# Dense layer with squared ReLU on one core: the blocks in another order, and two small weight loads on another queue

## The chip, the cores and the metric

The kernel runs on one core of one Trainium2 chip. The metric is device time in microseconds (us). "Before" had 293.56 us (median of 3 runs, 293.25 to 294.12) when the prediction was made.

## The reference

For x of 2048 x 576, w1 of 576 x 4608 and w2 of 4608 x 576, all bfloat16:

```python
h = jnp.einsum("bsd,df->bsf", x, w1) + b1
r = jnp.where(h > 0, h, 0)
h = r * r
out = jnp.einsum("bsf,fd->bsd", h, w2) + b2
```

## The kernel before

The 2048 rows are taken in four blocks of 512. For a block, stage A computes h transposed (36 column tiles of 128), and stage B multiplies it with w2. The contraction of A is 576 = 4.5 x 128. So 32 of the 36 tiles use **row-tiled** matmuls: the 128 rows of the array are two halves of 64, and two matmuls (a *pair*, lines 173 and 175) run side by side. The other four tiles use **full-array** matmuls (line 194) and a small row-tiled remainder (lines 188 and 190), whose weights are `w1n8`. B is full-array (line 233). In the profile's lines `w1_h`, the weights of the row-tiled tiles, appears as `w_h`, `w1n8` as `w1n_89` and the transposed x as `xTw`; PE are TensorE's matmuls, PEld its weight loads, DVE is VectorE, ACT ScalarE, POOL GpSimd. Before the first full-array matmul, TensorE runs seven warm-up matmuls and twenty small ones that transpose block 0 of x.

```python
    def load_w1n8(eng, h):                                   # 32 KB each
        src = w1[NK * P:D, 0:GW].rearrange("p (i h f) -> p i h f", h=2, f=P)
        keep(eng.dma_start(out=w1n8[h * H:(h + 1) * H, :, :], in_=src[:, :, h, :]))
    ...
    for k in range(NK):
        load_w1n(nc.sync, k)
    load_w1n8(nc.sync, 0)
    load_w1n8(nc.sync, 1)
    ...
    def a_full(sb, order):
        ...                      # "rows_first": remainder pairs, then the full-array groups
        ...                      # otherwise: full-array groups, then the remainder pairs
    ...
    for (j0, j1) in [(0, 1), (1, 2), (2, 4), (4, 6), (6, 8), (8, 10), (10, 12)]:
        load_w1(nc.sync, 0, j0, j1)          # upper halves of w_h, then lower halves
        load_w1(nc.sync, 1, j0, j1)
    load_xT(1)
    for (j0, j1) in [(12, 14), (14, 16)]:
        load_w1(nc.sync, 0, j0, j1)
        load_w1(nc.sync, 1, j0, j1)
    ...
    for c in (0, 3, 1, 4, 2, 5):
        load_w2(c)
    load_xT(2)

    alloc_hT(0)
    a_full(0, "k_outer")
    a_rows(0, 12, 1)
    alloc_hT(1)
    load_xT(3)
    a_rows(1)
    a_full(1, "rows_first")
    phase_b(0, hTs[0], dups=(2, 3))
    alloc_hT(2)
    a_full(2, "g_outer")
    a_rows(2)
    phase_b(1, hTs[1])
    alloc_hT(3)
    a_full(3, "g_outer")
    a_rows(3)
    phase_b(2, hTs[2])
    phase_b(3, hTs[3], last=True)
```

## Time and profile before

| what | before |
|---|---|
| span of the profiled run | 291.4 us |
| TensorE busy | 286.5 us, 98% |
| ScalarE, VectorE busy | 32%, 28% |
| first full-array matmul starts | 5.46 us |
| last matmul ends | 287.70 us |
| from there to the end of the span | 3.67 us |

The page of before, parts 1 (busy us, share of the span, instructions) and 4 (the chain of waits that ended last, by engine and by line):

```profile
PE 286.5 (98%) x2412; PEld 177.5 (61%) x2412; DVE 81.4 (28%) x189; ACT 93.7 (32%) x154; POOL 1.5 (1%) x8
...
PE 98%; ACT 0%; DVE 0%; issue 0%
```

TensorE has work nearly all the time, and the chain is its own sequence of matmuls.

The windows view of before gives one stage per line. Columns: stretch, its length, then busy time and instructions for each engine, granted clock, DMA share, GB/s. In order: blocks 0 and 1 of stage A, block 2 of A, block 3 of A, and what follows the last matmul.

```profile
5.46:76.07 70.61, 70.58 (x618) 31.39 (x619) 32.64 (x75) 45.10 (x73) 0.00 (x0) 1.00 0.83 174
...
111.35:146.51 35.16, 35.16 (x310) 15.60 (x307) 15.30 (x36) 21.32 (x34) 0.00 (x0) 1.00 0.02 6
...
181.80:216.97 35.17, 35.17 (x310) 15.60 (x308) 15.29 (x36) 21.32 (x34) 0.00 (x0) 1.00 0.02 5
...
287.70:291.37 3.67, 0.00 (x1) 0.00 (x0) 0.46 (x1) 0.00 (x0) 0.00 (x0) 0.91 0.07 22
```

Blocks 2 and 3 of A take 70.33 us together. They run apart, with a stage B between them.

The timeline of before, PE only (start, duration, line, operation), at a change from row-tiled to full-array and at one from row-tiled to stage B:

```profile
72.08 0.38 PE L188 MATMUL pn<-xTw,w1n_89 64*128 64x512 bf16 x1
72.29 0.38 PE L190 MATMUL pn<-xTw,w1n_89 64*128 64x512 bf16 x1
72.60 0.39 PE L194 MATMUL pn<-xTw,w1n 128*128 128x512 bf16 x1
...
146.20 0.38 PE L173 MATMUL ph<-xTw,w_h 64*128 64x512 bf16 x1
146.21 0.38 PE L175 MATMUL ph<-xTw,w_h 64*128 64x512 bf16 x1
146.51 0.30 PE L233 MATMUL po<-w_sb,hT 128*128 128x288 bf16 x1
```

Read the starts, not the durations, since matmuls overlap. Two starts of one half of the array are normally 0.215 us apart; across a change of mode it is 0.31 us.

The same view at the one visible wait for a weight load:

```profile
13.17 0.38 PE L173 MATMUL ph<-xTw,w_h 64*128 64x512 bf16 x1
13.18 0.38 PE L175 MATMUL ph<-xTw,w_h 64*128 64x512 bf16 x1
13.39 0.38 PE L173 MATMUL ph<-xTw,w_h 64*128 64x512 bf16 x1
13.79 0.39 PE L175 MATMUL ph<-xTw,w_h 64*128 64x512 bf16 x1
13.80 0.39 PE L173 MATMUL ph<-xTw,w_h 64*128 64x512 bf16 x1
```

At 13.39 one half of the array starts and its partner waits until 13.79.

The timeline of before, queue of SyncE (SPq), start and time over which the issues ran:

```profile
1.65 1.85 SPq L73 DMA_DIRECT2D w1n<-in_w_dram  x4
3.68 1.36 SPq L77 DMA_DIRECT2D w1n_89<-in_w_dram  x2
5.08 9.13 SPq L80 DMA_DIRECT2D w_h<-in_w_dram  x11
```

The two remainder loads take 1.36 us of issuing ahead of the first w_h load.

### The profile page before, as it was taken

What the parts mean: (1) busy time and instruction counts of PE and PEld (TensorE: products, weight loads), DVE (VectorE), ACT (ScalarE), POOL (GpSimd) and SP (SyncE); (2) the same over time, 40 slices, a digit from 0 to 9 for tenths busy, and PEclk for the clock granted to TensorE, in tenths of its full rate; (3) what the DMA queues carried; (4) which work ended last, traced back from release to release, by engine and by line L of the source; (5) the groups of instructions that cost most, each with busy time, mean ns of one, the idle gap of its engine ahead of it and who ended that gap; (6) DMA issues with size and microseconds to landing.
All of it is one profiled execution on the core that took longest, in us unless ns stands there. A gap on an engine that the chain in (4) does not pass through costs nothing.

```text
span 291.4 us, 5457 instructions
## 1 busy us (share of the span) xinstructions
PE 286.5 (98%) x2412; PEld 177.5 (61%) x2412; DVE 81.4 (28%) x189; ACT 93.7 (32%) x154; POOL 1.5 (1%) x8
## 2 busy tenths in 40 slices
PE   8999999999999999999999999999999999999994
PEld 4444444444687875444477877444457878777783
DVE  3444544444531011544411110344440111110110
ACT  4666666666400001766620000466660000000000
POOL 2000000000000000000000000000000000000000
PEclk9999999999999999999999999999999999999999
DMA  6999999900000000000000000000000000000000
GB/s 183 201 200 175 233 358 326 158 7 2 0 23 0 23 20 20 2 1 2 2 0 20 23 3 20 20 2 0 2 0 2 20 24 20 23 0 23 20 23 21
DMA packets 27320, 16.05 MB, mean 55 GB/s; under 512 B 11284, under 2 KB 27296, under 8 KB 27296
## 3 DMA queue, kind: packets, MB, share of 16 engines
q1 hardware_dynamic: 26976, 15.39, 23.2%
q8 instruction: 19, 0.31, 0.4%
q10 hardware_dynamic: 288, 0.30, 0.3%
q14 instruction: 5, 0.04, 0.0%
q0 software_dynamic: 32, 0.01, 0.0%
HBM read 11.36 MB, written 2.36 MB: 47 GB/s over the span
## 4 chain that ended last, share of the span: by engine, by line
PE 98%; ACT 0%; DVE 0%; issue 0%
PE po L233 49%; PE ph L173 23%; PE ph L175 20%; PE pn L194 5%; PE wps L61 1%; PE pn L188 1%; ACT xTw L143 0%; ACT xTw L144 0%; DVE o_sb L242 0%; PE pn L190 0%; PE ta L138 0%; PE tb L141 0%; PE tb L142 0%; PE b1T_ps L151 0%
## 5 line engine op out<-in xcount | busy, mean ns | idle before, releaser
L233 PE MATMUL po<-w_sb,hT 128*128 128x288 bf16 x1152 | 141.6, 286 | 0.0
L233 PEld LDWEIGHTS <-hT 128*128 128x128 bf16 x1152 | 112.6, 98 | 29.3 <-issue 0.8
L175 PE MATMUL ph<-xTw,w_h 64*128 64x512 bf16 x576 | 125.0, 376 | 0.0
L173 PE MATMUL ph<-xTw,w_h 64*128 64x512 bf16 x576 | 125.0, 376 | 0.0
L161 ACT ACTIVATE r<-ph,b1T 128x512 bf16<-128x512 f32 x128 | 81.1, 685 | 41.0 <-PE ph L173 20.5
L162 DVE TENSOR_TENSOR hT<-r 128x512 bf16<-128x512 bf16 x144 | 61.2, 425 | 79.3 <-ACT r L161 79.3
L173 PEld LDWEIGHTS <-w_h 64*128 64x128 bf16 x576 | 54.0, 94 | 36.4
L175 PEld LDWEIGHTS <-w_h 64*128 64x128 bf16 x576 | 54.0, 94 | 32.3 <-DMA w_h<-in_w_dram 0.8
L242 DVE TENSOR_TENSOR o_sb<-po,b_bc 128x288 bf16<-128x288 f32 x32 | 13.2, 453 | 122.5 <-PE po L233 122.5
L161 ACT ACTIVATE r<-pn,b1T 128x512 bf16<-128x512 f32 x16 | 10.0, 688 | 80.9 <-PE pn L190 80.1
L194 PE MATMUL pn<-xTw,w1n 128*128 128x512 bf16 x64 | 14.5, 379 | 0.4 <-ACT xTw L144 0.4
L194 PEld LDWEIGHTS <-w1n 128*128 128x128 bf16 x64 | 6.1, 98 | 7.6 <-DMA w1n<-in_w_dram 0.6
L61 PE MATMUL wps<-const-bfloat16-1.0 128*128 128x512 bf16 (+1 forms) x7 | 2.9, 593 | 0.8 <-PEq L306 0.8
L113 DVE COPY xTw<-xTw 64x2048 bf16<-64x2048 bf16 x4 | 2.8, 688 | 0.5 <-ACT xTw L144 0.4
L114 DVE COPY xTw<-xTw 64x2048 bf16<-64x2048 bf16 x4 | 2.8, 688 | 0.1
L188 PE MATMUL pn<-xTw,w1n_89 64*128 64x512 bf16 x8 | 2.4, 380 | 0.0
L190 PE MATMUL pn<-xTw,w1n_89 64*128 64x512 bf16 x8 | 2.4, 380 | 0.0
L139 DVE COPY xTw<-ta 128x384 bf16<-128x384 bf16 x4 | 1.2, 358 | 4.1 <-PE ta L138 4.1
L61 PEld LDWEIGHTS <-const-bfloat16-1.0 128*128 128x128 bf16 x7 | 0.9, 135 | 2.1 <-issue 2.1
L98 ACT ACT_TABLE_LOAD x1 | 1.3, 1283 | 1.7 <-PEq L306 1.7
L143 ACT COPY xTw<-tb 128x128 bf16<-128x128 bf16 x4 | 1.2, 298 | 1.1 <-PE tb L142 1.1
L138 PE MATMUL ta<-ident,x_sb 128*128 128x128 bf16 x12 | 1.4, 240 | 0.0
(20 smaller groups left out, 8.4 us busy)
## 6 DMA issues: line engine op xcount, KB each, us to landing
w_sb<-in_w_dram SPq DMA_DIRECT2D x6, 864.0 KB, 11.5
w_h<-in_w_dram SPq DMA_DIRECT2D x14, 288.0 KB, 6.7
out_dram<-o_sb SPq DMA_DIRECT2D x15, 144.0 KB, 1.8
w_h<-in_w_dram SPq DMA_DIRECT2D x4, 144.0 KB, 3.4
w1n<-in_w_dram SPq DMA_DIRECT2D x4, 128.0 KB, 3.3
x_sb<-in_x_dram ACTq DMA_DIRECT2D x2, 144.0 KB, 3.1
x_sb<-in_x_dram SPq DMA_DIRECT2D x2, 144.0 KB, 2.8
b_bc<-in_b_dram SPq DMA_DIRECT2D x1, 144.0 KB, 6.1
```

What stands on the lines that cost most here:

```text
L61: keep(nc.tensor.matmul(wps[:, 0:n], lhsT=ones[:, 0:P], rhs=ones[:, 0:n], start=True, stop=True))
L113: keep(nc.vector.tensor_copy(out=xT[0:H, SPC:SPC + 4, :], in_=xT[H:P, E3:E3 + 4, :]))
L114: keep(nc.vector.tensor_copy(out=xT[H:P, SPC:SPC + 4, :], in_=xT[0:H, O:O + 4, :]))
L161: keep(nc.scalar.activation(out=r[:], in_=bank[:], func=ACT.Relu, bias=b1T[:, ft:ft + 1], scale=1.0))
L162: keep(nc.vector.tensor_tensor(out=hTs[sb][:, ft, :], in0=r[:], in1=r[:], op=ALU.mult))
L173: keep(nc.tensor.matmul(bx[:], lhsT=w1_h[0:H, LO_C[i], jc], rhs=xT[0:H, LO_W[i], :], start=(i == 0), stop=(i == NC - 1)))
L175: keep(nc.tensor.matmul(by[:], lhsT=w1_h[H:P, UP_C[i], jc], rhs=xT[H:P, UP_W[i], :], start=(i == 0), stop=(i == NC - 1)))
L188: keep(nc.tensor.matmul(banks[2 * i][:], lhsT=w1n8[0:H, i, :], rhs=xT[0:H, SPC, :], start=start, stop=stop))
L190: keep(nc.tensor.matmul(banks[2 * i + 1][:], lhsT=w1n8[H:P, i, :], rhs=xT[H:P, E3, :], start=start, stop=stop))
L194: keep(nc.tensor.matmul(banks[g][:], lhsT=w1n[:, k, g * P:(g + 1) * P], rhs=xT[:, O + k, :], start=start, stop=stop))
L233: keep(nc.tensor.matmul(po[h][:, 0:DH], lhsT=hT[:, ft, jj * P:(jj + 1) * P], rhs=w2_sb[:, ft, h * DH:(h + 1) * DH], start=(i == 0), stop=( ...
L242: keep(nc.vector.tensor_tensor(out=o_sb[:, h * DH:(h + 1) * DH], in0=po[h][:, 0:DH], in1=b2_bc[:, h * DH:(h + 1) * DH], op=ALU.add,))
```

## The change

The intent: blocks go A0 A1 B0 B1 A2 A3 B2 B3, so that the row-tiled parts of A2 and A3 meet and full-array work stands at every border to stage B. That is four changes of tiling mode instead of six. The two remainder loads go to the GpSimd queue, so that w_h can be issued earlier.

```diff
-    load_w1n8(nc.sync, 0)
-    load_w1n8(nc.sync, 1)
 ...
     nc.gpsimd.dma_start(out=b1_rows[0:NFT, :], in_=b1.rearrange("(ft p) -> ft p", p=P))
+    load_w1n8(nc.gpsimd, 0)
+    load_w1n8(nc.gpsimd, 1)
 ...
     phase_b(0, hTs[0], dups=(2, 3))
+    phase_b(1, hTs[1])
     alloc_hT(2)
     a_full(2, "g_outer")
     a_rows(2)
-    phase_b(1, hTs[1])
     alloc_hT(3)
-    a_full(3, "g_outer")
     a_rows(3)
+    a_full(3, "rows_first")
     phase_b(2, hTs[2])
```

## The prediction

> **What bounds the kernel now.** TensorE. The busy table has PE at 286.5 us of a 291.4 us span (98%), and the chain of waits is 98% PE: second phase (L233) 49%, row-tiled first phase (L173/L175) 43%, full-array first phase (L194) 5%. Clock granted 0.999. In the timeline the matmul starts follow without holes: 0.215 us for each full 512-column matmul and for each row-tiled pair, 0.122 us for each 288-column one. ACT (32%) and DVE (28%) have slack. The change keeps all 2412 matmuls, so only holes count.
>
> **Holes that the timeline shows.**
> 1. Changes between row-tiled (64x128) and full-array matmuls. Last row pair of A1 at 72.29, first full one at 72.60: 0.31 us against 0.215. The same 0.31 us from full to row in A0, A2 and A3 (185.04 to 185.35), and from the rows of A2 and A3 to phase B (146.21 to 146.51; 216.66 to 216.97). Each is 0.095 us too long, and the next one or two starts are some 0.01 us late: about 0.10 us a change, six changes in all. Between full groups and phase B nothing is lost. This agrees with the Trainium skill, "TensorEngine Tiling (Array Packing)", Key Properties: changing the tiling mode drains the engine.
> 2. One DMA wait: at 13.39 the next pair starts 0.40 us later, waiting for a w1 load (w_h), a loss of 0.19 us.
>
> **What the change does.**
> - Order. A2 full, rows, then A3 rows, full joins the two row parts and ends with full groups before B2. It removes three switches (A2 rows to B1; A3 full to rows; A3 rows to B2) and adds one (A3 rows to A3 full). Net two fewer: 2 x 0.10 = 0.20 us, all on the critical path. Nothing new waits: hT 3 reuses the buffer B1 has finished with, x blocks 2 and 3 are ready, and eviction (0.69 us each, two per 1.94 us of rows) keeps up as from A0 to A1.
> - Loads. The two 32 KB loads cost the sync queue 1.36 us of issue (3.68 to 5.04), ahead of the first w_h issue at 5.08. Without them w_h issues start about 1.4 us sooner. The Trainium skill, "DMA: Bandwidth & Descriptors", says that issuing engines share the same 16 DMA engines and that spreading only saves issue time; issue time is what is saved here. I expect the wait at 13.39 to go: -0.19 us. On the GpSimd queue the loads are issued after the b1 load (1.45, 0.66 us), at about 2.1 and 3; with the b1 load's 3.5 us to landing they are there by about 7, needed at 9.06.
>
> **Sum.** -0.20 - 0.19 = -0.39 us of 293.56: predicted 293.2 us, range 292.6 to 293.8 (runs of before spread over 0.9 us). Chances: faster by over 2% 0.005, within 2% 0.99, slower 0.005.
>
> **What would show it.** Four 0.31 us steps in the PE timeline instead of six, none at the end of A2's rows or into B2; no w_h wait in the list of waits; w_h issues starting near 3.7.
>
> **What would make it wrong.** The loads through GpSimd landing after 9, so that the first remainder pairs wait (the wait list would name w1n_89); a wait of A3's closing full groups on PSUM banks; x or w1n arriving later because 256-byte pieces compete with them; or run-to-run scatter hiding so small a gain.

## The result

Changed kernel: 292.49 us median (6 runs, 292.06 to 292.75). Before in the same rounds: 293.64 us (6 runs, 293.25 to 294.32). The ratio is 0.9955, 95% interval 0.994 to 0.997. Ratios here and below are worked out from the fast runs of the same rounds; they are not quite the ratios of the medians quoted. The class "within 2%" was right; the gain of 1.15 us is three times the predicted 0.39 us, and the time lies below the range.

The windows view of the changed kernel, for the same stages (A0 and A1; A2 and A3; after the last matmul):

```profile
5.71:75.90 70.19, 70.03 (x616) 31.44 (x618) 32.67 (x75) 45.05 (x72) 0.00 (x0) 1.00 0.86 175
...
146.46:216.61 70.15, 69.94 (x617) 31.38 (x617) 30.63 (x72) 44.89 (x71) 0.00 (x0) 1.00 0.01 3
...
287.33:290.34 3.01, 0.00 (x1) 0.00 (x0) 0.46 (x1) 0.00 (x0) 0.00 (x0) 1.00 0.09 27
```

The two profiled spans differ by 1.03 us. By the stamps of the traces, in us to the nearest ns, this is:

| part | before | changed | difference |
|---|---|---|---|
| start to the first full-array matmul | 5.460 | 5.708 | +0.25 |
| A0 and A1 | 70.606 | 70.196 | -0.41 |
| A2 and A3 | 70.334 | 70.143 | -0.19 |
| B0 to B3 | 141.304 | 141.284 | -0.02 |
| last matmul to the end | 3.666 | 3.010 | -0.66 |

The wait of w_h near 13.4 us is gone from A0 and A1. At the same place as in before the pairs of the changed kernel follow each other without a hole:

```profile
13.42 0.38 PE L173 MATMUL ph<-xTw,w_h 64*128 64x512 bf16 x1
13.43 0.38 PE L175 MATMUL ph<-xTw,w_h 64*128 64x512 bf16 x1
13.64 0.38 PE L173 MATMUL ph<-xTw,w_h 64*128 64x512 bf16 x1
```

More than half of the difference comes after the last matmul, where the change seems to do nothing. The last instructions of the program's own work look the same in both. Timelines, first of before, then of the changed kernel:

```profile
287.74 0.46 DVE L242 TENSOR_TENSOR o_sb<-po,b_bc 128x288 bf16<-128x288 f32 x1 [3.95 <-PE po L233]
288.23 0.33 SPq L254 DMA_DIRECT2D out_dram<-o_sb  x1
```
```profile
287.37 0.46 DVE L242 TENSOR_TENSOR o_sb<-po,b_bc 128x288 bf16<-128x288 f32 x1 [3.95 <-PE po L233]
287.86 0.33 SPq L254 DMA_DIRECT2D out_dram<-o_sb  x1
```

The list of waits of the SyncE queue shows a difference in the closing code (line 317, the end of the program's context): waited in total, times, longest. First before, then changed:

```profile
SPq L317 <- DMA out_dram<-o_sb: 1.2, 1, 1.2
```
```profile
SPq L317 <- DMA out_dram<-o_sb: 0.4, 1, 0.4
```

The wait for the last output DMA is shorter, yet that DMA does not land sooner: its last semaphore increment comes 2.10 us after the last matmul's end in before and 2.11 us in the changed kernel. So something else ran first. The raw records of the two traces show it. SyncE closes with a list of semaphore waits, one or two semaphores an entry (a listing made from the records, start and end in us):

```
before:  last output DMA on semaphore 102     changed: last output DMA on semaphore 109
288.604  288.621  S103                        288.246  288.263  S102
288.664  289.827  S104 and S102               288.310  288.338  S103 and S100
290.279  290.307  S106 and S100               288.380  288.408  S104 and S112
290.352  290.380  S107 and S110               288.450  288.478  S106 and S111
290.421  290.449  S108 and S118               288.917  288.945  S107 and S110
290.483  290.511  S109 and S105               288.990  289.018  S108 and S118
                                              289.455  289.483  S109 and S105
```

An entry costs about 0.07 us, and one in each list (106 and 100 in before, 107 and 110 in the changed kernel) starts some 0.45 us late for a reason that no record shows. In before, the DMA that lands last is asked for in the second entry, so the rest of the list comes *after* its landing (289.80): the last entry starts 0.68 us later, and 0.45 us of that are the late entry. In the changed kernel it is asked for in the last entry, which waits for it and starts at 289.455, 0.02 us after the landing at 289.44. The rest of the list, its late entry too, ran while the DMA was under way. Why another semaphore: the records of these two traces show the DMAs of the SyncE and ScalarE queues taking eight semaphores in rotation (100, 102, 103, 104, 106, 107, 108, 109). The change takes two DMAs out of that rotation, so the last one moves two places back, from the second (102) to the eighth (109).

The theory (T) is thus three effects: fewer mode changes, 0.21 us; an earlier w_h, of uncertain size; and the end, 0.66 us, as a side effect of the *number* of hardware DMAs. The rivals: the shorter end is chance (R1), or comes of the new order (R3), or of using the GpSimd queue (R4).

### The profile page after: what moved, and what is told of

The parts are those of the page before. It is cut to its first block, busy times and chain, and to the rows that moved or that the text cites. A ratio compares the mean times of both kernels' runs of the same rounds, so it can differ in the third digit from the quotient of the medians.

```text
span 290.3 us, 5455 instructions
## 1 busy us (share of the span) xinstructions
PE 285.7 (98%) x2409; PEld 178.0 (61%) x2412; DVE 81.5 (28%) x189; ACT 94.2 (32%) x154; POOL 2.7 (1%) x10
## 4 chain that ended last, share of the span: by engine, by line
PE 98%; ACT 0%; issue 0%; DVE 0%
PE po L233 49%; PE ph L173 42%; PE pn L194 5%; PE wps L61 1%; PE ph L175 1%; PE pn L188 1%; PE ta L138 0%; ACT xTw L143 0%; DVE o_sb L242 0%; ACT xTw L144 0%; PE tb L141 0%; PE tb L142 0%; PE b1T_ps L151 0%; PE pn L190 0%
```

## The experiments

Eleven runs were made, of eight new kernels and of three repeats of before and the changed kernel, and every one gave the right result. They ran in three sets of rounds; before, in the same rounds, had a median of 293.77 us for the first four, 293.60 us for the next four and 293.49 us for the last three.

### Only the loads

The changed kernel with the old order of blocks.

```diff
-    load_w1n8(nc.sync, 0)
-    load_w1n8(nc.sync, 1)
+    load_w1n8(nc.gpsimd, 0)      # both behind the b1 load
+    load_w1n8(nc.gpsimd, 1)
```

> Order of the kernel before; only the two w1 remainder loads go to the GpSimd queue. Theory T (two separate effects of the loads: the w_h wait goes, worth 0.41 us of the first two row stages, and the last output DMA moves to the semaphore that the closing list of waits asks for last, worth 0.66 us after the last matmul): 1.05 us below before, about 292.6 us; last matmul to end of span 3.0 us, as in the changed kernel (before: 3.67). Rival R1 (the shorter end is chance from run to run): 0.41 us below before at most, end near 3.67 again or anywhere between. Rival R2 (my prediction: the wait costs 0.19): 0.2 us below before. Six changes of tiling mode stay, so 0.2 us of the change must be missing here.

Measured: 292.69 us, ratio 0.9961 (0.9944 to 0.9977), so 1.08 us below before by the medians. The end took 3.01 us, the last output DMA was on semaphore 109, and there was no w_h wait. A2 and A3 took 70.334 us, as in before. T holds for this run. The loads give most of the gain, so R3 has no room left, and R2, my own prediction (0.2 us), falls.

### Only the order

> Only the new order of blocks; loads stay on the sync queue. T: four changes of mode in place of six, 0.2 us below before; the w_h wait near 13.4 us stays (a step of about 0.4 us inside a pair); the last DMA has the same semaphore as before, so last matmul to end of span stays near 3.67 us. R3 (the order itself shortens the end or gives most of the 1.15 us): 0.8 us or more below before, end near 3.0 us.

```diff
     phase_b(0, hTs[0], dups=(2, 3))
+    phase_b(1, hTs[1])
 ...                              # as in the change; the loads stay on nc.sync
```

Measured: 293.43 us, ratio 0.9985 (0.9968 to 1.0002). A2 and A3 took 70.143 us, B 141.284 us, and the end 3.67 us. R3 falls: the order gives 0.21 us in the trace and leaves the end alone. The interval includes 1, so the times alone show no gain by the order; the 0.34 us of the medians does not contradict the trace. This run waited twice for w_h. Its timeline of the weight-load engine (PEld) shows the wait near 14 us and a second one that I had not expected; the bracket is the idle time before the line, and what ended it:

```profile
14.08 0.09 PEld L175 LDWEIGHTS <-w_h 64*128 64x128 bf16 x1 [0.60 <-DMA w_h<-in_w_dram]
33.85 0.09 PEld L175 LDWEIGHTS <-w_h 64*128 64x128 bf16 x1 [0.67 <-DMA w_h<-in_w_dram]
```

### Two DMAs fewer, by merging w_h loads

```diff
-    for (j0, j1) in [(12, 14), (14, 16)]:
-        load_w1(nc.sync, 0, j0, j1)
-        load_w1(nc.sync, 1, j0, j1)
+    load_w1(nc.sync, 0, 12, 16)
+    load_w1(nc.sync, 1, 12, 16)
```

> The kernel before, with the last two late pairs of w_h loads merged into one pair of twice the size: two DMAs fewer on the hardware queues, nothing else. The eight DMA semaphores are used in rotation, so the last output DMA moves from the second of them to the eighth, which the closing list of waits asks for in its last entry. T: last matmul to end of span 3.0 us instead of 3.67, time 0.66 us below before, the w_h wait near 13.4 and the six mode changes as before. R1 (chance) or R4 (the shorter end comes of the GpSimd queue): end near 3.67, same time as before.

Measured: 296.40 us, ratio 1.0085. The time was a miss: I had taken these loads to be early enough, and they are not. The larger pieces land later: the merged load of the half that waits landed at 35.70 us, while in before the first of its two parts had landed at 33.16 us. The list of waits shows it:

```profile
PEld L175 <- DMA w_h<-in_w_dram: 3.2, 2, 2.8
```

One step of each half of the array, from about 33.1 us on, took 2.66 us. But the end took 3.005 us, with the last DMA on semaphore 109, and no load had gone to GpSimd. So the end followed the rotation, and the time did not test it.

### The changed kernel with two DMAs more

```diff
-    for c in (0, 3, 1, 4, 2, 5):
+    for c in (0, 3, 1, 4, 2):
         load_w2(c)
+    for c0 in (30, 32, 34):
+        keep(nc.sync.dma_start(out=w2_sb[:, c0:c0 + 2, :], in_=w2_view[:, c0:c0 + 2, :]))
```

> The changed kernel, with the last w2 load cut into three: two hardware DMAs more, so the last output DMA is back on the second semaphore, which here stands in the first entry of the closing list (the list has two entries more pairs than before by the two GpSimd loads). T: all the other entries, some 0.07 us each with one gap of some 0.4 us among them, then come after the landing: end 3.7 to 3.9 us instead of 3.0, time 0.7 to 0.9 us above the changed kernel, that is 0.2 to 0.45 us below before. R1 or R4: end near 3.0, time as the changed kernel, 1.15 us below before.

Measured: 293.25 us, ratio 0.9978 (0.9961 to 0.9994). The end took 3.83 us, inside the expected 3.7 to 3.9, with the last DMA on 102 in the first entry of the list. (The list has seven entries, one more than before, not two: the two GpSimd loads add two semaphores to it.) The wait list of its SyncE queue (its closing code is line 319):

```profile
SPq L319 <- DMA out_dram<-o_sb: 1.3, 1, 1.3
```

R1 and R4 fall: the loads are still on GpSimd, and two more DMAs took the shorter end away. The median lies 0.52 us below before, slightly more than I expected (0.2 to 0.45), within the interval.

### Two DMAs fewer, by cutting w2 into four

```diff
-    W2CH = 6
+    W2CH = 9
-    for c in (0, 3, 1, 4, 2, 5):
+    for c in (0, 2, 1, 3):
```

> The kernel before, with w2 loaded in four pieces of nine row blocks in place of six of six: two hardware DMAs fewer, in a part of the load (31 to 60 us, needed after 76 us) that no matmul waits for. It repeats the test of the two merged w_h loads without their stall. T: the last output DMA is on the eighth semaphore; last matmul to end of span 3.0 us instead of 3.67; time 0.66 us below before; row stages and mode changes as before. R4 (the shorter end needs the GpSimd queue): end 3.67, same time as before.

Measured: 293.07 us, ratio 0.9985 (0.9972 to 0.9998). The end took 3.008 us, the last DMA was on 109, and A2 and A3 took 70.333 us. The windows view of what follows the last matmul:

```profile
288.14:291.15 3.01, 0.00 (x0) 0.00 (x0) 0.46 (x1) 0.00 (x0) 0.00 (x0) 1.00 0.09 27
```

This is the clean form of the test: the kernel before with nothing but two late loads fewer is faster, by 0.53 us of the medians, and the end is the only part of its profile that is shorter, by more than 0.001 us, than in both profiles of before. (0.66 us of 293.60 is a ratio of 0.9978, inside the interval.)

### The loads on the ScalarE queue

```diff
-    load_w1n8(nc.sync, 0)
-    load_w1n8(nc.sync, 1)
+    load_w1n8(nc.scalar, 0)
+    load_w1n8(nc.scalar, 1)
```

> The kernel before, with the two remainder loads issued by the ScalarE queue: the sync queue is relieved as in the change, but they stay hardware DMAs in the same place of the rotation. T: w_h issues start near 3.7 us and the wait near 13.4 us goes (-0.4 us), while the last output DMA keeps the second semaphore, so the end stays 3.67 us; the ScalarE table load comes some 1.3 us later, which may move the first full-array matmul by up to 0.3 us. So 0.1 to 0.4 us below before. R5 (relieving the sync queue shortens the end of the kernel too): end near 3.0 us and about 1 us below before.

Measured: 293.22 us, ratio 0.9989 (0.9977 to 1.0001). The interval includes 1. The end took 3.69 us, so R5 falls: relieving the SyncE queue does not shorten it. One expectation missed: w_h issues began at 4.73 us, not near 3.7, and a wait of 0.25 us near 13.6 stayed. The list of waits of its SyncE queue says why:

```profile
SPq L73 <- DMA x_sb<-in_x_dram: 0.9, 1, 0.9
SPq L80 <- DMA x_sb<-in_x_dram: 0.4, 1, 0.4
```

In the traces of before and of this kernel each hardware DMA from the ninth on waits until the earlier one on the same semaphore has landed. The rotation, here over 100 and 102 to 108, thus also bounds how many hardware DMAs are out at once, and here the x loads held the weights back.

### Second looks at both kernels

> The kernel before once more, for a second profile: which parts of the difference repeat. T: end 3.67 us; six changes of mode of 0.31 us; at least one w_h wait in the first two row stages, of a size that may differ (the kernel with only the new order showed a second one near 33 us, so the loss by these waits may lie between 0.4 and 1.0 us); first full-array matmul anywhere between 5.4 and 5.8 us, by chance. R1 would have the end differ.

> The changed kernel once more, for a second profile. T: end 3.0 us; four changes of mode; no w_h wait; first full-array matmul anywhere between 5.4 and 5.8 us, so that the 0.25 us by which it came later in the first profile is chance. If the start is again at 5.7 us or later, the loads on the GpSimd queue may have delayed it.

Measured, one run each, of unknown state: 293.83 us and 293.29 us. The ends were 3.67 and 3.03 us, and A2 and A3 took 70.334 and 70.143 us: these two terms repeat to 0.02 us. The start and the w_h waits do not, and what was expected of them missed. The first full-array matmul began at 6.42 us in before (5.46 the first time) and at 6.35 us in the changed kernel (5.71). Before had no w_h wait at all this time; the changed kernel had one near 34 us:

```profile
34.11 0.09 PEld L175 LDWEIGHTS <-w_h 64*128 64x128 bf16 x1 [0.52 <-DMA w_h<-in_w_dram]
```

By the expectation a start at 5.7 us or later would have pointed to the GpSimd loads, but before, without them, started later still, so these two starts decide nothing. The late starts come with slow transposes: starts of transposes are 0.107 us apart at first and 0.056 us later. In the first profile of before the step down came at about 4.0 us, in that of the changed kernel at about 4.5 us; in the second look at before it had not come by the last transpose, at 5.78 us. (The second also had its first transpose 0.25 us later, at 3.78 us, as x landed later.) The 0.25 us of the first pair of profiles go with this: VectorE's last copy of transposed x ended at 5.31 us in before and at 5.56 us in the changed kernel, and the first full-array matmul started 0.15 us after it in both.

### Order and end without moving the loads, against the changed kernel

This combines the new order with w2 in four pieces; the loads stay on SyncE. Apart from the size of the w2 pieces, it differs from the changed kernel in what the loads do at the start.

```diff
+    (the new order of blocks)
-    W2CH = 6
+    W2CH = 9
-    for c in (0, 3, 1, 4, 2, 5):
+    for c in (0, 2, 1, 3):
```

> The new order of blocks and w2 in four pieces; the remainder loads stay on the sync queue. Order (0.21 us) and end (3.0 us, last DMA on the eighth semaphore) are then those of the changed kernel, so this kernel differs from it in nothing but the earlier w_h issues. T: 0.87 us below before (0.21 + 0.66) by these two alone; what is still missing to the changed kernel of the same rounds is what the loads gave at the start: 0.2 to 0.5 us by the runs so far (first full-array matmul and w_h waits scatter by several tenths from run to run). R6 (moving the loads gives nothing at the start, all of it was chance): equal to the changed kernel within 0.1 us.

> The changed kernel, in the same rounds as the one with the loads on the sync queue. T: 1.15 us below before again, end 3.0 us, A2 to B3 0.21 us shorter than before, and 0.2 to 0.5 us below that other kernel. R6: equal to it within 0.1 us.

Measured: 292.64 us, ratio 0.9974 (0.9960 to 0.9987), and for the changed kernel 292.54 us, ratio 0.9966 (0.9954 to 0.9979). The changed kernel lies 0.95 us below before by the medians, where 1.15 was expected. Both ends took 3.013 us. The medians are 0.10 us apart and the means 0.19 us, with five runs each that spread over 0.6 to 0.7 us. What the loads give at the start is too small to be shown by this: R6 is neither confirmed nor refuted. Order and end together give 0.85 us of the medians, where T said 0.87.

### The late w_h loads ahead of the x transposes

```diff
-    load_xT(1)
     for (j0, j1) in [(12, 14), (14, 16)]:
         ...
+    load_xT(1)
 ...
-    a_rows(0, 12, 1)
+    a_rows(0, 14, 1)
```

> The changed kernel, with the last two pairs of w_h loads issued ahead of the transposing x load of block 1 instead of behind it, and that block's copies made two row groups later. Aimed at the w_h wait near 33 us, which two of the nine profiles of kernels with unmerged loads show (0.41 and 0.55 us). T: no wait near 33 in any run; the mean gains only what the wait cost on average, 0 to 0.2 us below the changed kernel, which these rounds can hardly show; end 3.0 us as there. If block 1 arrives too late for its copies, evictions stall and the time is above the changed kernel.

The 0.41 and 0.55 us named there are whole steps; counted as losses they are 0.42 us (on the half that waits longer) and 0.35 us in the table below.

Measured: 292.64 us, ratio 0.9968 (0.9956 to 0.9981), the same as the changed kernel (292.54) within the scatter. Its one profile has no wait near 33 us, while the changed kernel of the same rounds had one of 0.50 us. A single profile does not show that the wait is gone for good. No version was found that beats the changed kernel.

### All profiles side by side

Each line is one profiled run; "to B0" is the start of the first stage-B matmul, all times in us. The kernel with the merged w_h loads is left out of the comparison of "to B0" because of its own wait.

| kernel | w1n8 loads on | first full matmul | lost to w_h near 13 | near 33 | to B0 | A2 + A3 | end |
|---|---|---|---|---|---|---|---|
| before | SyncE | 5.46 | 0.41 | - | 76.07 | 70.334 | 3.67 |
| before, second | SyncE | 6.42 | - | - | 76.75 | 70.334 | 3.67 |
| only the order | SyncE | 5.67 | 0.49 | 0.35 | 76.70 | 70.143 | 3.67 |
| merged w_h loads | SyncE | 5.61 | 0.32 | 2.46 | 78.59 | 70.335 | 3.01 |
| w2 in four | SyncE | 6.17 | 0.14 | - | 76.50 | 70.333 | 3.01 |
| order, w2 in four | SyncE | 6.23 | - | - | 76.43 | 70.143 | 3.01 |
| loads on ScalarE | ScalarE | 5.65 | 0.26 | - | 76.10 | 70.334 | 3.69 |
| changed | GpSimd | 5.71 | - | - | 75.90 | 70.143 | 3.01 |
| changed, second | GpSimd | 6.35 | - | 0.42 | 76.96 | 70.143 | 3.03 |
| changed, third | GpSimd | 5.76 | - | 0.50 | 76.47 | 70.144 | 3.01 |
| only the loads | GpSimd | 5.74 | - | - | 75.94 | 70.334 | 3.01 |
| changed, two DMAs more | GpSimd | 5.60 | 0.11 | 0.02 | 75.95 | 70.143 | 3.83 |
| late w_h first | GpSimd | 6.17 | - | - | 76.37 | 70.143 | 3.02 |

A loss is counted on the half of the array that waits: its steps over the usual 0.216 us. Near 13 us it is 0.32 to 0.49 us in the three SyncE kernels that started early (5.46 to 5.67), at most 0.14 us in the three that started late, and at most 0.11 us in the six with the loads on GpSimd. A late start gives the loads time, so start and wait partly cancel. The mean of "to B0" is 76.26 us over the six GpSimd profiles and 76.49 us over the five SyncE ones, with ranges of 75.90 to 76.96 and 76.07 to 76.75: 0.2 us apart, and not settled.

Two things set the first full-array matmul. One is the transposes: in the eight profiles that start before 5.8 us their steps are short by 4.7 us, in the five that start after 6.1 us not before 5.3 us. The other is a risk that the prediction had named, w1n arriving later. The last of the four w1n loads landed at 6.64 to 7.58 us in the six GpSimd profiles and at 6.16 to 6.72 us in the six SyncE ones. In two GpSimd profiles the first full-array matmul had to wait for a w1n load: in the third look at the changed kernel the load landed at 5.71 us and the matmul started at 5.76 us, and with two DMAs more at 5.55 and 5.60 us. In the other eleven the matmul starts 0.14 to 0.15 us after VectorE's last copy; by that these two are 0.30 and 0.15 us late, an estimate. The timeline of the third look:

```profile
5.76 1.47 PE L194 MATMUL pn<-xTw,w1n 128*128 128x512 bf16 x6 [0.73 <-DMA w1n<-in_w_dram]
```

So moving the loads can also cost something at the start.

## Why the prediction was wrong

1. **What bounds the kernel: right.** TensorE at 98%, and the gain was bounded by small holes.
2. **Mode changes: right.** Predicted 0.20 us for two fewer. Measured 0.19 us in A2 and A3 and 0.02 us in the two stages B that followed row-tiled work. All kernels with the new order have 70.143 to 70.144 us, all others 70.333 to 70.335 us. Row-tiled work now runs through the border of A2 and A3, as this part of the changed timeline shows (starts 0.215 us apart, no 0.31):

```profile
181.32 0.38 PE L173 MATMUL ph<-xTw,w_h 64*128 64x512 bf16 x1
181.32 0.38 PE L175 MATMUL ph<-xTw,w_h 64*128 64x512 bf16 x1
181.54 0.38 PE L173 MATMUL ph<-xTw,w_h 64*128 64x512 bf16 x1
181.54 0.38 PE L175 MATMUL ph<-xTw,w_h 64*128 64x512 bf16 x1
```

3. **Loads on time: right for the two loads, but the named risk to w1n came true in part.** The two remainder loads were issued at 2.16 and 2.76 us, had landed by 5.85 and 6.56 us, and were needed at 9.31 us. The first w_h issue moved to 3.61 us, as predicted ("near 3.7"):

```profile
3.61 10.95 SPq L80 DMA_DIRECT2D w_h<-in_w_dram  x12
```

The w1n loads, though, landed later, and two of six GpSimd profiles lost an estimated 0.30 and 0.15 us by it (see the side-by-side section).

4. **The wait of w_h: direction right, size wrong, and not fixed.** The prediction took "0.40 us later, waiting for a w1 load (w_h), a loss of 0.19 us". It subtracted a pair's 0.215 us from a step that lies *inside* a pair, where the normal distance is 0.003 us. The loss in that run was 0.40 us; A0 and A1 became 0.41 us shorter. The other profiles show that the wait is no constant, and that a second one near 33 us survives the change. The sign "no w_h wait in the list of waits" held in the first profile and failed in two repeats. On average the loads give perhaps 0.2 us at the start, which would be close to the predicted 0.19, but the runs don't settle it.
5. **The end: missing, and the step that failed.** The prediction said: "The change keeps all 2412 matmuls, so only holes count." It does not mention the 3.67 us after the last matmul, so it took them as fixed. In fact 0.66 us of them depended on how many hardware DMAs the program issues, since that decides where the last one's semaphore stands in the closing list. This was tested in both directions: two DMAs fewer shorten the end without GpSimd and without a new order, two more lengthen it in the changed kernel. It is the largest term of the gain.

The sum of what is shown is 0.21 + 0.66 = 0.87 us. The measured gain is 1.15 us by the medians of the first rounds and 0.95 us in the last ones (293.49 - 292.54); the 0.1 to 0.3 us that remain would be the start, of which the runs show only that it scatters; how much of them the loads gave stays open. The Trainium skill, "TensorE: Matmul & The Clock Gate", Part 1, says that the array clock rises only after some time of activity, and that the moment varies from run to run because the activity window runs freely. The transposes agree: their steps go from 0.107 to 0.056 us at a different time in almost every profile, and in two they are short from the first transpose, at 3.5 us.

## What to carry to other kernels

When a kernel is bound by one engine at 98%, read the microseconds before its first and after its last instruction as carefully as the holes, and compare the records there, since a change in the count of DMAs can move them. Take such terms from several profiles: two of the terms here repeat to 0.02 us, and the start scatters by almost 1 us: the first pair of profiles has the changed kernel start 0.25 us later, the second 0.07 us earlier. A step between two instructions is a loss only beyond *its own* normal distance; look up which neighbours normally stand how far apart before subtracting.

## What the Trainium skill lacked or had wrong

- No page that I read has the closing list of semaphore waits. An entry took about 0.07 us, one of them started 0.45 us late, and whether the last DMA's semaphore came early or last in the list made 3.67 us or 3.01 us of the time after the last matmul (3.83 us with the longer list of the changed kernel). "Runtime: NRT & Kernel Launch" tells of barriers and resets after a kernel, not of this list.
- "TensorEngine Tiling (Array Packing)", Key Properties, states that changing the tiling mode drains the engine, without a size. The runs show 0.31 us from start to start instead of 0.215 us, and 0.21 us for two changes.
- "DMA: Bandwidth & Descriptors", Issuing engines are not separate DMA queues, is right that what is saved is issue time (first w_h issue at 3.61 us instead of 5.08 us), but adds nothing on a limit seen here: a hardware DMA of this program waits for the earlier landing on the same one of eight semaphores, which held back the SyncE queue by 0.9 and 0.4 us when the loads were issued from ScalarE.
- "TensorE: Matmul & The Clock Gate", Part 1, gives about 4 us of sustained activity, give or take 0.5 us from run to run, for the clock to rise; it also says that the window runs freely. Here the scatter is wider than 0.5 us. Matmuls began at 0.78 us; by the steps of the transposes the rise came by 3.5 us in two profiles, at about 4.0 us in the first one of before and after 5.78 us in the second, so from at most 2.7 us to over 5.0 us later. The activity was not unbroken (how soon x landed moved the first transpose from 3.5 to 3.8 us), so this is no test of the 4 us themselves.
